# Attention scores computed by slot, with block transposes on VectorE, in a fused attention and two expert networks

## The chip, the cores and the metric
The kernel runs on one core of one Trainium2 chip. The metric is the device time of one execution in microseconds (us), the median of several runs.

## The reference
All inputs come in float32 but for the weights, which are float64; what is computed is this:

```python
a = phi - np.max(phi, axis=2, keepdims=True)          # phi: (8, 8, 576, 32)
a = np.exp(a); a = a / (np.sum(a, axis=2, keepdims=True) + 1e-09)
k_m = np.einsum('bhsm,bhsd->bhmd', a, k)              # k, v, q: (8, 8, 576, 64)
v_m = np.einsum('bhsm,bhsd->bhmd', a, v)
scores = np.matmul(q, k_m.transpose(0, 1, 3, 2)) / np.sqrt(64)
scores = scores - np.max(scores, axis=-1, keepdims=True)
attn = np.exp(scores)
attn = attn / (np.sum(attn, axis=-1, keepdims=True) + 1e-09)
x = np.matmul(attn, v_m)                              # tokens 4608 x 512
g = x @ w_gate
x = (g / (1 + np.exp(-g)) * (x @ w_val)) @ w_out      # 512 -> 1536 -> 512
h = x @ w_in                                          # 512 -> 2048 -> 512
out = np.where(h > 0, h, np.exp(np.minimum(h, 0)) - 1) @ w2_out
```

There are 8 batches of 8 heads, 576 tokens, head size 64 and 32 memory slots. For each head k and v are first pooled into 32 slots (k_m, v_m); the softmax over the slots is the attention.

## The kernel before
The program has three stages. Stage 1 goes over the batches; in each it computes units 0 to 3 of the first expert network (a unit is 128 of the 1536 hidden columns), in two halves of 288 tokens (HS). Stage 2 does units 4 to 11 of all batches, stage 3 the second expert network. The attention is spread over stage 1 only. v_m is never multiplied with the attention: it is folded into the gate and value weights (`vw`, L139, eight matmuls on 64x32 tiles of the array), so the gate and value matmuls (`gate1`, `val1`, L151 to L153) take the normalised scores `at`, split in a high and a low part. `down1` is L156 to L158. VectorE makes s (L176) and h (L183) from their PSUM tiles, which release the three banks of `ps_gv`, and the low part hl (L164).

The attention of a batch has two parts.
- `front_tasks`: `phi` (max L216 on VectorE, exp on ScalarE L219), `a_T` (transposes of the exponentials, by TensorE, L234, copied by ScalarE L236), `kv_mm` (L247: the products with k and v; two groups g of four heads j, each head a 32-column strip of the array, over five chunks of tokens of which the last has 64), `kv_out` (L255, the division by the sum) and `kv_T` (L263: transposes; ScalarE copies the v part to vt, L266, and the k part to kT, L271, into a tile padded with zeros by GpSimd, L270).
- `back_tasks`: `score` (L282: per chunk of 128 tokens and pair of heads one matmul with 128 tokens of q stationary and 64 columns of the padded kT moving; the result has tokens on partitions), max over slots L286, subtraction L287, exp L288, `norm` (sum L294, L295, reciprocal L296, product L297), and `attn_T` (L307: TensorE turns the normalised scores back to slots on partitions; ScalarE writes the high part, L310, VectorE the low part, L311). `score` and `norm` work on three pieces of two, two and one chunk, `attn_T` on two pieces.

In stage 1 the lists of tasks of later batches are worked off by `tick()` between gates, values and downs; ahead of it stand batch 0 and part of batches 1 and 2 in a prologue. A scheduler then sets the order on each engine. Every engine, and the DMA queue on SP, works in its own order; `together` keeps a group of matmuls next to each other. Weights come in float64 and are split by ScalarE (L100, L107), VectorE (L101 to L105) and GpSimd (L108 to L111). The buffers that count here: `ps_at` has two PSUM banks for scores and their transposes, `ps_fr` one, `kvr` six chunks (NKV), `qr` six chunks (NQ).

Of the kernel before, what the change touches and what calls it, by code (L numbers as in the profile page):

```python
# [37 lines left out]
def attention_moe_moe(ctx: ExitStack, tc: tile.TileContext, qT, phiT, kv, w1g, w1o, w2, out):
# [148 lines left out]
    ident = bk_p.tile([128, 128], F32, tag="ident", name="ident")  # L187
    make_identity(nc, ident)

    def chunk(c):  # L190
        return min(128, S - 128 * c)

    class Batch:
        def __init__(self, b):
# [5 lines left out]
            nc.sync.dma_start(out=self.ph, in_=phiT[self.b].rearrange("g p s -> p g s"))  # L200

        def load_kv(self, c):
            n = chunk(c)
            t = self.kvr[c] = fr_p.tile([128, 2, 512], F32, tag="kvr", name="kvr", bufs=NKV)
            nc.sync.dma_start(out=t[:n], in_=kv[self.b, 128 * c:128 * c + n])

        def load_q(self, c):
            n = chunk(c)
            t = self.qr[c] = bk_p.tile([128, 512], F32, tag="qr", name="qr", bufs=NQ)
            nc.sync.dma_start(out=t[:, :4 * n], in_=qT[self.b, :, 512 * c:512 * c + 4 * n])  # L210


        def phi(self):
# [8 lines left out]
            nc.vector.tensor_scalar_add(out=self.rs, in0=sm, scalar1=1e-9)  # L222
            nc.vector.reciprocal(out=self.rs, in_=self.rs)

        def a_T(self, c0):
# [2 lines left out]
            n = chunk(c0)
            nch = 2 if n == 128 else 1
            ps = ps_fr.tile([128, 2, 256], F32, tag="at", name="ps_aT")  # L230
            for i in range(nch):
                for g in range(2):
                    s0 = 128 * (c0 + i)
                    nc.tensor.transpose(out=ps[:n, i, 128 * g:128 * g + 128],  # L234
                                        in_=self.ph[:, g, s0:s0 + n], identity=ident)
            act(out=self.a[:n, c0:c0 + nch], in_=ps[:n, :nch], func=AF.Copy)  # L236


        def kv_mm(self, cs, start, stop):
            if start:  # L240
                self.kvp = [ps_kv.tile([128, 2, D], F32, tag="at", name="ps_kvm") for _ in range(2)]

            def head(c, g, j):
                n = chunk(c)
                t = self.kvr[c].rearrange("p t (j g d) -> p t g j d", j=4, g=2)
                o = 128 * g + 32 * j
                return mm(self.kvp[g][32 * j:32 * j + 32], lhsT=self.a[:n, c, o:o + 32], rhs=t[:n, :, g, j, :],  # L247
                          start=start and c == cs[0], stop=stop and c == cs[-1])
# [9 lines left out]
        def kv_T(self):  # L260
# [6 lines left out]
            self.kT = bk_p.tile([128, 4, 2, M], F32, tag="kT", name="kT", bufs=2)
            for g in range(2):
                r, o = slice(64 * g, 64 * g + 64), slice(64 - 64 * g, 128 - 64 * g)
                nc.gpsimd.memset(self.kT[o, :, g, :], 0.0)  # L270
                act(out=self.kT[r, :, g, :], in_=ps[r, 0], func=AF.Copy)  # L271


        def score(self, c0, c1):
            if c0 == 0:
                self.sc = bk_p.tile([128, NCH, 256], F32, tag="sc", name="sc")
            n, k = chunk(c0), (c1 - c0) * 8
            ps = ps_at.tile([128, 2, 2, 4, M], F32, tag="at", name="ps_sc")
            for c in range(c0, c1):
                q = self.qr.pop(c)[:, :4 * n].rearrange("p (j s) -> p j s", j=4)  # L280
                for j in range(4):
                    mm(ps[:n, c - c0, :, j, :], lhsT=q[:, j, :], rhs=self.kT[:, j], start=True, stop=True)  # L282
            p = ps[:n, :c1 - c0].rearrange("p c g j m -> p (c g j) m")
            sc = self.sc[:n, c0:c1, :].rearrange("p c (h m) -> p (c h) m", m=M)
            mx = bk_p.tile([128, 16, 1], F32, tag="mx", name="mx", bufs=2)[:n, :k]
            nc.vector.tensor_reduce(out=mx, in_=p, op=ALU.max, axis=AX.X)  # L286
            tt(out=sc, in0=p, in1=mx.to_broadcast([n, k, M]), op=ALU.subtract)  # L287
# [2 lines left out]
        def norm(self, c0, c1):  # L290
            n, k = chunk(c0), (c1 - c0) * 8
            sc = self.sc[:n, c0:c1, :].rearrange("p c (h m) -> p (c h) m", m=M)
            sm = bk_p.tile([128, 16, 1], F32, tag="smx", name="smx", bufs=2)[:n, :k]
# [3 lines left out]
            tt(out=sc, in0=sc, in1=sm.to_broadcast([n, k, M]), op=ALU.mult)  # L297

        def attn_T(self, c0, c1):
            if c0 == 0:  # L300
# [1 line left out]
            s0, s1 = 128 * c0, min(S, 128 * c1)
            for g in range(2):
                ps = ps_at.tile([128, 512], F32, tag="at", name="ps_atT")[:, :s1 - s0]
                for c in range(c0, c1):
                    n = chunk(c)
                    nc.tensor.transpose(out=ps[:, 128 * (c - c0):128 * (c - c0) + n],  # L307
                                        in_=self.sc[:n, c, 128 * g:128 * g + 128], identity=ident[:n, :n])
                hi, lo = self.at[:, 0, g, s0:s1], self.at[:, 1, g, s0:s1]
                a = act(out=hi, in_=ps, func=AF.Copy)  # L310
                self.mark = a, tt(out=lo, in0=ps, in1=hi.bitcast(F32), op=ALU.subtract)  # L311
# [19 lines left out]

    def back_tasks(b):
        z, nxt = Bs[b], Bs[b + 1] if b + 1 < B else None
        yield lambda: (z.score(0, 2), nxt and [nxt.load_q(c) for c in (0, 1)])
        yield lambda: (z.score(2, 4), nxt and [nxt.load_q(c) for c in (2, 3)])
        yield lambda: (z.score(4, 5), nxt and nxt.load_q(4), 0 < b < B - 2 and Bs[b + 2].phi())
        yield lambda: z.norm(0, 2)
        yield lambda: (z.attn_T(0, 2), setattr(z, 'mark1', z.mark))
        yield lambda: (z.norm(2, 4), z.norm(4, 5))
        yield lambda: (z.attn_T(2, 5), z.store_at())  # L340
# [276 lines left out]
```

## Time and profile before

| | us |
|---|---|
| median of 3 runs (lowest, highest) | 1632.61 (1631.53, 1634.37) |
| the profiled execution | 1629.19 |
| its span, first to last instruction | 1627.4 |
| TensorE busy | 1577.3 (97%) |
| VectorE busy | 962.4 (59%) |
| ScalarE busy | 659.3 (41%) |
| GpSimd busy | 169.4 (10%) |

The mean granted clock of TensorE is 0.982 of full speed. How to read it: the busy shares are means over three stages with different limits; what lies ahead of about 330 us holds all of the attention, and what follows has none. Busy time of TensorE counts overlapping matmuls once; the time of a group of matmuls is read from its start to the start of the next instruction. One fp32 matmul leaves two records in the trace.

### The profile page before, as it was taken

The numbers are of one execution on the slowest core, as the hardware profiler recorded it, in microseconds if no ns is written. First come the engines' busy times: TensorE is split into PE (matmuls) and PEld (weight loads), VectorE is DVE, ScalarE is ACT, GpSimd is POOL, SyncE is SP. The second block draws the span as 40 slices with busy tenths as digits, with TensorE's granted clock in tenths as the row PEclk, the third lists the DMA queues.
The fourth block names the chain that finished last, engine by engine and source line by source line (L and its number), as shares of the span: only waits on it lengthen the run. The fifth ranks groups of instructions, "written<-read, shape, count | busy, mean of one in ns | idle before, by whom it ended". The sixth has DMA issues, their size and how long they took to land.

```text
span 1627.4 us, 24651 instructions
## 1 busy us (share of the span) xinstructions
PE 1577.3 (97%) x9968; PEld 1358.8 (83%) x9968; DVE 962.4 (59%) x1718; ACT 659.3 (41%) x1281; POOL 169.4 (10%) x135
## 2 busy tenths in 40 slices
PE   6699999999999999999999999999999999999998
PEld 4588888888999999999987788888888888888887
DVE  5778777665444544443799755555555555555554
ACT  3455444454333333333455443434343434343333
POOL 1211111132011010100244200000000000000000
PEclk7699999999999999999999999999999999999999
DMA  8877443243222322221242010101010101010000
GB/s 300 272 251 251 166 140 133 76 167 108 73 94 82 101 74 83 85 87 45 87 149 91 34 33 0 52 1 52 1 52 1 52 0 53 1 52 0 26 1 26
DMA packets 65906, 136.34 MB, mean 84 GB/s; under 512 B 6912, under 2 KB 38656, under 8 KB 63744
## 3 DMA queue, kind: packets, MB, share of 16 engines
q1 hardware_dynamic: 56576, 125.32, 23.0%
q10 hardware_dynamic: 9216, 9.44, 1.7%
q8 instruction: 78, 1.28, 0.3%
q14 instruction: 36, 0.29, 0.1%
HBM read 96.99 MB, written 37.75 MB: 83 GB/s over the span
## 4 chain that ended last, share of the span: by engine, by line
PE 80%; DVE 9%; DMA 7%; ACT 2%; issue 1%; SPq 0%; ACTq 0%; DVEq 0%
PE pu L534 7%; PE pu L535 7%; PE pu L533 7%; PE acc L559 7%; PE acc L560 7%; PE acc L561 7%; PE acc L156 4%; PE acc L158 4%; PE acc L157 4%; PE pg L151 3%; PE pv L151 3%; PE pvw L139 3%; PE pg L153 3%; PE pg L152 3%; PE pv L152 2%; PE pv L153 2%
## 5 line engine op out<-in xcount | busy, mean ns | idle before, releaser
L561 PE MATMUL acc<-whi,hl 128*128 128x512 f32 x576 | 222.5, 391 | 2.8 <-DVE hl L164 2.8
L559 PE MATMUL acc<-whi,hh 128*128 128x512 f32 x576 | 224.3, 389 | 0.1
L560 PE MATMUL acc<-wlo,hh 128*128 128x512 f32 x576 | 224.1, 389 | 0.0
L533 PE MATMUL pu<-x1s,whi 128*128 128x512 f32 x576 | 224.1, 389 | 0.0
L534 PE MATMUL pu<-x1s,whi 128*128 128x512 f32 x576 | 224.1, 389 | 0.0
L535 PE MATMUL pu<-x1s,wlo 128*128 128x512 f32 x576 | 224.1, 389 | 0.0
L548 DVE SCALAR_TENSOR_TENSOR g<-e,g 128x512 f32<-128x512 f32 x144 | 103.7, 720 | 159.2 <-ACT g L547 159.2
L162 ACT ACTIVATE hh<-g 128x512 fp32r<-128x512 f32 x144 | 91.0, 632 | 212.8 <-DVE g L549 209.4
L183 DVE SCALAR_TENSOR_TENSOR h<-s,pv 128x288 f32<-128x288 f32 x192 | 86.5, 450 | 146.5 <-PE pv L153 132.5
L546 ACT ACTIVATE e<-g 128x512 f32<-128x512 f32 x144 | 90.8, 631 | 202.8 <-DVE g L545 202.8
L164 DVE TENSOR_TENSOR hl<-g,hh 128x512 fp32r<-128x512 f32 x144 | 101.1, 702 | 88.5 <-ACT hh L162 88.4
L156 PE MATMUL acc<-hh,whi 128*128 128x288 f32 x512 | 151.3, 296 | 0.1
L157 PE MATMUL acc<-hh,wlo 128*128 128x288 f32 x512 | 150.5, 294 | 0.0
L158 PE MATMUL acc<-hl,whi 128*128 128x288 f32 x512 | 149.5, 295 | 0.0
L162 ACT ACTIVATE hh<-h 128x288 fp32r<-128x288 f32 x192 | 85.0, 443 | 153.1 <-DVE h L183 152.6
L164 DVE TENSOR_TENSOR hl<-h,hh 128x288 fp32r<-128x288 f32 x192 | 94.5, 492 | 65.0 <-ACT hh L162 65.0
L561 PEld LDWEIGHTS acc<-whi,hl 128*128 128x128 f32 x576 | 108.0, 188 | 28.5 <-DVE hl L164 6.2
L559 PEld LDWEIGHTS acc<-whi,hh 128*128 128x128 f32 x576 | 108.2, 188 | 22.7 <-ACT hh L162 0.5
L534 PEld LDWEIGHTS pu<-x1s,whi 128*128 128x128 f32 x576 | 108.3, 188 | 22.4
L560 PEld LDWEIGHTS acc<-wlo,hh 128*128 128x128 f32 x576 | 108.0, 188 | 22.4
L533 PEld LDWEIGHTS pu<-x1s,whi 128*128 128x128 f32 x576 | 108.1, 188 | 22.3
L535 PEld LDWEIGHTS pu<-x1s,wlo 128*128 128x128 f32 x576 | 108.1, 188 | 22.3
(85 smaller groups left out, 3281.2 us busy)
## 6 DMA issues: line engine op xcount, KB each, us to landing
kvr<-kv SPq DMA_DIRECT2D x32, 512.0 KB, 7.5
wr<-w SPq DMA_DIRECT2D x32, 512.0 KB, 3.5
wr<-w1g SPq DMA_DIRECT2D x24, 512.0 KB, 4.7
atd<-at SPq DMA_DIRECT2D x8, 1152.0 KB, 4.7
p1d<-p ACTq DMA_DIRECT2D x64, 144.0 KB, 1.8
p1l<-p1d SPq DMA_DIRECT2D x16, 576.0 KB, 4.2
at<-atd SPq DMA_DIRECT2D x8, 1152.0 KB, 5.2
x1d<-p1l SPq DMA_DIRECT2D x16, 576.0 KB, 3.3
```

Source lines behind the costliest of these rows:

```text
L156: mm(ps, lhsT=w[0][:, ms], rhs=hs[0], start=start, stop=False)
L157: mm(ps, lhsT=w[1][:, ms], rhs=hs[0], start=False, stop=False)
L158: mm(ps, lhsT=w[0][:, ms], rhs=hs[1], start=False, stop=stop)
L162: act(out=hh, in_=h, func=AF.Copy)
L164: tt(out=hl, in0=h, in1=hh.bitcast(F32), op=ALU.subtract)
L533: mm(ps, lhsT=wh[:, k, :], rhs=xh, start=k == 0, stop=False)
L534: mm(ps, lhsT=wh[:, k, :], rhs=xl, start=False, stop=False)
L535: mm(ps, lhsT=wl[:, k, :], rhs=xh, start=False, stop=k == KD - 1)
L548: stt(out=g, in0=e, scalar=1.0, in1=g, op0=ALU.add, op1=ALU.mult)
L559: mm(accs[c], lhsT=hs[0][:, cs], rhs=wh, start=u == 0, stop=False)
L560: mm(accs[c], lhsT=hs[0][:, cs], rhs=wl_, start=False, stop=False)
L561: mm(accs[c], lhsT=hs[1][:, cs], rhs=wh, start=False, stop=u == NU2 - 1)
```

## The change
- `score` works by half (288 tokens) in place of by chunk. Now kT of a head is stationary (64 x 32) and q moves with 288 columns: eight heads lie side by side on eight 64x32 tiles of the array, into two PSUM tiles with slots on partitions. kT is no longer padded.
- VectorE turns the scores in blocks of 32x32 into an SBUF tile (two instructions of 128x288 a half), then max, subtraction, exp, sum, reciprocal and product run on 128x576; one more block transpose of 128x576 turns them back (into `ex`), and the high and low parts come from there. `attn_T` with its TensorE transposes is gone.
- The second group of phi comes rolled by 64 tokens, so the last 64 tokens of both groups share one transpose and one tile; the last 64 tokens of k and v come packed (`kv4`), so their eight matmuls are on 64x32 tiles.
- The loop of `kv_mm` has j outside and g inside, where g was outside.
- NKV is 5 (and two small `kv4` buffers), NQ is 3 halves; two transfers of q a batch in place of five; `back_tasks` has six tasks in place of seven.

```diff
-NKV = 6
-NQ = 6
+NKV = 5
+NQ = 3
...
         def a_T(self, c0):
             if c0 == 0:
-                self.a = fr_p.tile([128, NCH, 256], F32, tag="a", name="a")
...
+                self.a = fr_p.tile([128, 9, 128], F32, tag="a", name="a")
+            ps = ps_fr.tile([128, 4, 128], F32, tag="at", name="ps_aT")
+            ph = self.ph.rearrange("p g s -> p (g s)")
+            if c0 == 4:
+                nc.tensor.transpose(out=ps[:, 0], in_=ph[:, 512:640], identity=ident)
+                act(out=self.a[:, 8], in_=ps[:, 0], func=AF.Copy)
+                return
...
             def head(c, g, j):
...
+                if c < 4:
+                    a = self.a[:, 2 * c + g, col]
+                    t = self.kvr[c].rearrange("p (t j g d) -> p g j t d", t=2, j=4, g=2)[:, g, j]
+                else:
+                    r = slice(64 * g, 64 * g + 64)
+                    a, t = self.a[r, 8, col], self.kvr[c][r].rearrange("p (t j d) -> p j t d", t=2, j=4)[:, j]
+                return mm(self.kvp[g][col], lhsT=a, rhs=t, start=start and c == cs[0], stop=stop and c == cs[-1])
...
-            together([lambda c=c, g=g, j=j: head(c, g, j) for c in cs for g in (1, 0) for j in range(4)])
+            together([lambda c=c, g=g, j=j: head(c, g, j) for c in cs for j in range(4) for g in (1, 0)])
...
+        def score(self, hf):
+            q = self.qr.pop(hf)
+            ps = [ps_at.tile([128, HS], F32, tag="at", name="ps_sc") for _ in range(2)]
+
+            def head(j, g):
+                r = slice(64 * g, 64 * g + 64)
+                return mm(ps[g][32 * j:32 * j + 32], lhsT=self.kT[r, j, :], rhs=q[r, j, :], start=True, stop=True)
+
+            together([lambda j=j, g=g: head(j, g) for j in range(4) for g in (1, 0)])
+            t = self.sc = bk_p.tile([128, 2, HS], F32, tag="sc", name="sc", bufs=2)
             for g in range(2):
...
+                nc.vector.transpose(out=t[:, g], in_=ps[g])
+            sc = t.rearrange("p g (b m) -> p (g b) m", m=M)
+            mx = bk_p.tile([128, 2 * HS // M, 1], F32, tag="mx", name="mx", bufs=2)
+            nc.vector.tensor_reduce(out=mx, in_=sc, op=ALU.max, axis=AX.X)
+            tt(out=sc, in0=sc, in1=mx.to_broadcast([128, 2 * HS // M, M]), op=ALU.subtract)
             act(out=sc, in_=sc, func=AF.Exp, scale=1.0 / float(D) ** 0.5)
...
+        def attn(self, hf):
+            if hf == 0:
                 self.at = av_p.tile([128, 2, 2, S], F32R, tag="at", name="at")
...
+            t = bk_p.tile([128, 2, HS], F32, tag="ex", name="ex")
+            nc.vector.transpose(out=t.rearrange("p g s -> p (g s)"), in_=self.sc.rearrange("p g s -> p (g s)"))
+            hi, lo = (self.at[:, i, :, HS * hf:HS * hf + HS] for i in range(2))
+            a = act(out=hi, in_=t, func=AF.Copy)
+            self.mark = a, tt(out=lo, in0=t, in1=hi.bitcast(F32), op=ALU.subtract)
```

The order on the engines shows how the work moves at two places. On TensorE, between the pooling of batch 1 and the first gate (L139 at the end is the second vw group of batch 0; the first gate follows it), there stood before:

```order
L139 MATMUL pvw<-wg,vt 32x512 x8
L263 MATMUL ps_kvT<-ident,kvm 128x128 x2
L234 MATMUL ps_aT<-ident,ph 128x128 x4
L282 MATMUL ps_sc<-kT,qr 128x2x32 x11
L234 MATMUL ps_aT<-ident,ph 128x128 x4
L282 MATMUL ps_sc<-kT,qr 128x2x32 x5
L282 MATMUL ps_sc<-kT,qr 64x2x32 x4
L234 MATMUL ps_aT<-ident,ph 64x128 x2
L247 MATMUL ps_kvm<-kvr,a 32x128 x40
L307 MATMUL ps_atT<-ident,sc 128x128 x4
L139 MATMUL pvw<-wg,vt 32x512 x8
```

And now:

```order
L265 MATMUL ps_kvT<-ident,kvm 128x128 x2
L139 MATMUL pvw<-wg,vt 32x512 x8
L280 MATMUL ps_sc<-qr,kT 32x288 x8
L235 MATMUL ps_aT<-ident,ph 128x128 x4
L280 MATMUL ps_sc<-qr,kT 32x288 x8
L235 MATMUL ps_aT<-ident,ph 128x128 x4
L229 MATMUL ps_aT<-ident,ph 128x128
L251 MATMUL ps_kvm<-kvr,a 32x128 x40
L265 MATMUL ps_kvT<-ident,kvm 128x128 x2
L280 MATMUL ps_sc<-qr,kT 32x288 x8
L235 MATMUL ps_aT<-ident,ph 128x128 x4
L139 MATMUL pvw<-wg,vt 32x512 x8
```

The scores of batch 1 are two groups of eight in place of twenty matmuls in pieces, L307 is gone, and the kv transposes, half of the scores and four of the transposes of the next batch now stand ahead of the first gate.

On VectorE, at the softmax of batch 1 (L101 to L105 are the splitting of weights), there stood before:

```order
L286 TENSOR_REDUCE mx<-ps_sc 128x16
L287 TENSOR_TENSOR sc<-ps_sc,mx 128x512
L101 TENSOR_SCALAR wc<-wv 128x512
L102 SCALAR_TENSOR_TENSOR wv<-wv,wc 128x512
L294 TENSOR_REDUCE smx<-sc 128x16
L104 TENSOR_SCALAR wc<-wv 128x512
L101 TENSOR_SCALAR wc<-wv 128x512
L295 TENSOR_SCALAR smx<-smx 128x16
L105 SCALAR_TENSOR_TENSOR wc<-wr,wc 128x512
L102 SCALAR_TENSOR_TENSOR wv<-wv,wc 128x512
L296 RECIPROCAL smx<-smx 128x16
L286 TENSOR_REDUCE mx<-ps_sc 128x16
```

And now:

```order
L285 STREAM_TRANSPOSE sc<-ps_sc 128x288 x2
L101 TENSOR_SCALAR wc<-wv 128x512
L288 TENSOR_REDUCE mx<-sc 128x18
L102 SCALAR_TENSOR_TENSOR wv<-wv,wc 128x512
L289 TENSOR_TENSOR sc<-sc,mx 128x576
L285 STREAM_TRANSPOSE sc<-ps_sc 128x288
L104 TENSOR_SCALAR wc<-wv 128x512
L285 STREAM_TRANSPOSE sc<-ps_sc 128x288
L101 TENSOR_SCALAR wc<-wv 128x512
L105 SCALAR_TENSOR_TENSOR wc<-wr,wc 128x512
L295 TENSOR_REDUCE smx<-sc 128x18
L288 TENSOR_REDUCE mx<-sc 128x18
```

The max no longer reads PSUM but the tile that two block transposes have filled; those alone release the score banks.

## Rows read from the trace of the kernel before

**Rows 1.** Windows: busy us (x count) by engine, granted clock, DMA share, GB/s.
```profile
core 0: us, PE busy (x) PEld busy (x) DVE busy (x) ACT busy (x) POOL busy (x), PEclk, DMA share, GB/s
60.00:80.00 20.00, 13.22 (x129) 9.42 (x128) 18.02 (x37) 8.82 (x21) 7.90 (x8) 0.68 0.77 246
80.00:100.00 20.00, 17.44 (x195) 14.97 (x194) 19.43 (x40) 9.85 (x24) 6.85 (x7) 0.91 0.80 278
120.00:320.00 200.00, 194.13 (x1649) 169.05 (x1648) 151.27 (x331) 93.55 (x218) 23.65 (x23) 0.99 0.46 155
220.00:240.00 20.00, 17.96 (x124) 14.39 (x117) 17.11 (x36) 9.23 (x21) 3.86 (x5) 0.91 0.34 115
420.00:1627.00 1207.00, 1197.62 (x6750) 1030.81 (x6748) 669.80 (x1106) 466.44 (x838) 94.52 (x62) 1.00 0.15 50
```

**Rows 2.** Waits of TensorE, 120 to 320 us: us in total, times, longest.
```profile
PE pd L156 <- DVE h L183: 3.7, 3, 2.0
```

**Rows 3.** Timeline of TensorE in the middle: start us, us, engine, line, form, count.
```profile
187.17 2.52 PE L247 MATMUL ps_kvm<-kvr,a 64*32 64x128 f32 x80
189.63 0.40 PE L156 MATMUL pd<-hh,whi 128*128 128x288 f32 x1
...
202.34 0.58 PE L307 MATMUL ps_atT<-ident,sc 128*128 128x128 f32 x3
202.85 0.40 PE L151 MATMUL pv<-at,vw 128*128 128x288 f32 x1
203.09 0.29 PE L152 MATMUL pv<-at,vw 128*128 128x288 f32 x1
...
206.75 1.00 PE L282 MATMUL ps_sc<-kT,qr 128*128 128x64 f32 x8
207.56 0.38 PE L151 MATMUL pv<-at,vw 128*128 128x288 f32 x1
207.78 0.29 PE L152 MATMUL pv<-at,vw 128*128 128x288 f32 x1
```

**Rows 4.** Timeline of TensorE around one vw group in stage 2.
```profile
419.76 0.29 PE L152 MATMUL pv<-at,vw 128*128 128x288 f32 x1
419.89 0.29 PE L153 MATMUL pv<-at,vw 128*128 128x288 f32 x1
420.12 1.09 PE L139 MATMUL pvw<-wg,vt 64*32 64x512 f32 x16
421.13 0.40 PE L156 MATMUL acc<-hh,whi 128*128 128x288 f32 x1
421.37 0.29 PE L157 MATMUL acc<-hh,wlo 128*128 128x288 f32 x1
```

**Rows 5.** Timeline of TensorE in the prologue.
```profile
18.42 8.14 PE L282 MATMUL ps_sc<-kT,qr 128*128 128x64 f32 x40 [1.95 <-ACT kT L271]
...
75.14 1.90 PE L307 MATMUL ps_atT<-ident,sc 128*128 128x128 f32 x6 [3.42 <-DVE at L311]
```

**Rows 6.** VectorE by line and form, 0 to 420 us: busy us, mean ns, idle before.
```profile
L286 DVE TENSOR_REDUCE mx<-ps_sc 128x16 f32<-128x512 f32 x16 | 10.9, 680 | 5.7 <-PE ps_sc L282 5.7
L311 DVE TENSOR_TENSOR at<-ps_atT,at 128x320 fp32r<-128x320 f32 x16 | 7.8, 488 | 1.5 <-ACT at L310 1.5
L311 DVE TENSOR_TENSOR at<-ps_atT,at 128x256 fp32r<-128x256 f32 x16 | 6.4, 417 | 1.2 <-ACT at L310 0.9 <-DMA p1d<-p 0.3
L255 DVE TENSOR_SCALAR kvm<-ps_kvm,rs 128x128 f32<-128x128 f32 x16 | 4.7, 328 | 7.1 <-PE ps_kvm L247 7.1
L286 DVE TENSOR_REDUCE mx<-ps_sc 64x8 f32<-64x256 f32 x8 | 3.3, 407 | 0.0
L296 DVE RECIPROCAL smx<-smx 64x8 f32<-64x8 f32 x8 | 1.4, 174 | 0.0
```

More of the change, by code (lines that the diff above doesn't have):

```diff
@@ L32, with attention_moe_moe @@
 NWC = 8
-NKV = 6
-NQ = 6
+NKV = 5
+NQ = 3
 @with_exitstack
-def attention_moe_moe(ctx: ExitStack, tc: tile.TileContext, qT, phiT, kv, w1g, w1o, w2, out):
+def attention_moe_moe(ctx: ExitStack, tc: tile.TileContext, qT, phiT, kv, kv4, w1g, w1o, w2, out):
     nc = tc.nc
@@ L188, in attention_moe_moe @@
     make_identity(nc, ident)
-    def chunk(c):
-        return min(128, S - 128 * c)
     class Batch:
@@ L202, in load_kv, with load_q @@
         def load_kv(self, c):
[L203 to L210, printed above, removed]
+            t = self.kvr[c] = fr_p.tile([128, 1024 if c < 4 else 512], F32, tag="kvr" if c < 4 else "kv4",
+                                        name="kvr", bufs=NKV if c < 4 else 2)
+            nc.sync.dma_start(out=t, in_=kv[self.b, 128 * c:128 * c + 128] if c < 4 else kv4[self.b])
+        def load_q(self, hf):
+            t = self.qr[hf] = bk_p.tile([128, 4, HS], F32, tag="qr", name="qr", bufs=NQ)
+            nc.sync.dma_start(out=t, in_=qT[self.b, hf].rearrange("p (j s) -> p j s", j=4))
         def phi(self):
@@ L226, in a_T @@
             if c0 == 0:
-                self.a = fr_p.tile([128, NCH, 256], F32, tag="a", name="a")
[L228 to L231, printed above, removed]
+                self.a = fr_p.tile([128, 9, 128], F32, tag="a", name="a")
[5 more added lines that the diff above has]
+                return
+            for i in range(2):
                 for g in range(2):
[L233 to L236, printed above, removed]
+                    s0 = 128 * (c0 + i) + 640 * g
+                    nc.tensor.transpose(out=ps[:, 2 * i + g], in_=ph[:, s0:s0 + 128], identity=ident)
+            act(out=self.a[:, 2 * c0:2 * c0 + 4], in_=ps, func=AF.Copy)
         def kv_mm(self, cs, start, stop):
@@ L243, in head @@
             def head(c, g, j):
[L244 to L248, printed above, removed]
-            together([lambda c=c, g=g, j=j: head(c, g, j) for c in cs for g in (1, 0) for j in range(4)])
+                col = slice(32 * j, 32 * j + 32)
+                if c < 4:
[6 more added lines that the diff above has]
+            together([lambda c=c, g=g, j=j: head(c, g, j) for c in cs for j in range(4) for g in (1, 0)])
         def kv_out(self):
@@ L264, in kv_T @@
                                     in_=self.kvm[:, i].rearrange("p g d -> p (g d)"), identity=ident)
+            self.kT = bk_p.tile([128, 4, M], F32, tag="kT", name="kT", bufs=2)
+            act(out=self.kT, in_=ps[:, 0], func=AF.Copy)
             self.vt = vt_p.tile([128, 4, M], F32, tag="vt", name="vt")
             act(out=self.vt, in_=ps[:, 1], func=AF.Copy)
[L267 to L271 removed]
@@ L274, in score @@
[L274 to L287, printed above, removed]
+        def score(self, hf):
[6 more added lines that the diff above has]
+            t = self.sc = bk_p.tile([128, 2, HS], F32, tag="sc", name="sc", bufs=2)
+            for g in range(2):
+                nc.vector.transpose(out=t[:, g], in_=ps[g])
[3 more added lines that the diff above has]
+            tt(out=sc, in0=sc, in1=mx.to_broadcast([128, 2 * HS // M, M]), op=ALU.subtract)
@@ L288, in score, with norm @@
             act(out=sc, in_=sc, func=AF.Exp, scale=1.0 / float(D) ** 0.5)
[L290 to L293, printed above, removed]
+        def norm(self, hf):
+            sc = self.sc.rearrange("p g (b m) -> p (g b) m", m=M)
+            sm = bk_p.tile([128, 2 * HS // M, 1], F32, tag="smx", name="smx", bufs=2)
@@ L296, in norm @@
             nc.vector.reciprocal(out=sm, in_=sm)
-            tt(out=sc, in0=sc, in1=sm.to_broadcast([n, k, M]), op=ALU.mult)
-        def attn_T(self, c0, c1):
-            if c0 == 0:
+            tt(out=sc, in0=sc, in1=sm.to_broadcast([128, 2 * HS // M, M]), op=ALU.mult)
+        def attn(self, hf):
+            if hf == 0:
                 self.at = av_p.tile([128, 2, 2, S], F32R, tag="at", name="at")
[L302 to L311, printed above, removed]
+            t = bk_p.tile([128, 2, HS], F32, tag="ex", name="ex")
[3 more added lines that the diff above has]
+            self.mark = a, tt(out=lo, in0=t, in1=hi.bitcast(F32), op=ALU.subtract)
         def store_at(self):
@@ L333, in back_tasks @@
         z, nxt = Bs[b], Bs[b + 1] if b + 1 < B else None
[L334 to L340, printed above, removed]
+        yield lambda: z.score(0)
+        yield lambda: (z.norm(0), nxt and nxt.load_q(0))
+        yield lambda: (z.attn(0), setattr(z, 'mark1', z.mark))
+        yield lambda: (z.score(1), 0 < b < B - 2 and Bs[b + 2].phi())
+        yield lambda: (z.norm(1), nxt and nxt.load_q(1))
+        yield lambda: (z.attn(1), z.store_at())
     G2 = [(ps_gv, "g")] * 2
@@ L355, in attention_moe_moe @@
         Bs[0].load_kv(c)
-    for c in range(NCH):
-        Bs[0].load_q(c)
+    for hf in range(2):
+        Bs[0].load_q(hf)
     Bs[0].phi()
@@ L593 @@
     gate, val = (inputs[n].reshape(KD, 128, NU1 // 2, 2, 1, 128) for n in ("moe_w_gate", "moe_w_val"))
+    ph = phi.reshape(B, 4, 2, S, M).transpose(0, 2, 1, 4, 3).reshape(B, 2, 128, S)
+    kvn = np.stack([a.transpose(0, 2, 1, 3).reshape(B, S, DM) for a in (k, v)], axis=2)
     arrays = {
-        "qT": np.concatenate([qT[..., c:c + 128].reshape(B, 128, -1) for c in range(0, S, 128)], axis=2),
-        "phiT": phi.reshape(B, 4, 2, S, M).transpose(0, 2, 1, 4, 3).reshape(B, 2, 128, S),
-        "kv": np.stack([k.transpose(0, 2, 1, 3).reshape(B, S, DM), v.transpose(0, 2, 1, 3).reshape(B, S, DM)], axis=2),
+        "qT": qT.reshape(B, 128, 4, 2, HS).transpose(0, 3, 1, 2, 4).reshape(B, 2, 128, 4 * HS),
+        "phiT": np.stack([ph[:, 0], np.roll(ph[:, 1], 64, axis=2)], axis=1),
+        "kv": kvn[:, :512].reshape(B, 512, 1024),
+        "kv4": kvn[:, 512:].reshape(B, 64, 2, 4, 2, D).transpose(0, 4, 1, 2, 3, 5).reshape(B, 128, 512),
         "w1g": np.concatenate([gate, val], axis=4).transpose(2, 0, 1, 3, 4, 5).reshape(NU1 // 2, KD, 128, 512),
```

## The prediction, made before the changed kernel ran
> **What bounds the kernel now.** I read the windows first. From 420 us to the end TensorE is busy 1197.62 of 1207 us [rows 1]: units 4 to 11 and the second expert network run there, the change touches nothing of them, and I take that stretch as fixed. All of the attention lies before about 330 us. In 120 to 320 us TensorE is busy 194.13 of 200 us and VectorE 151.27; so TensorE sets the pace there, and VectorE has 48.7 us to spare. The list of waits agrees: the largest wait of TensorE there is 3.7 us, for VectorE's h [rows 2]. Before 100 us it is otherwise. In 60 to 80 us TensorE is busy only 13.22 of 20 us and VectorE 18.02; in 80 to 100 us VectorE is busy 19.43; the transfers take 0.77 to 0.80 of their engines' time [rows 1]. So the prologue is paced by VectorE and the transfers, the middle by TensorE. TensorE work that goes is worth its full length in the middle and only a part of it in the prologue; VectorE work that comes costs little in the middle and much in the prologue.
>
> **TensorE, per batch.**
> Scores before: 40 records per batch (20 fp32 matmuls, two records each). Eight of them run from 206.75 to 207.56 us, 0.81 us, so 0.101 each [rows 3], 4.05 a batch; at half clock, batch 0 shows 8.14 us for 40 [rows 5]. They come in about six pieces, and behind a piece the first large matmul takes 0.22 us to the next one (207.56 to 207.78) and not 0.13: 0.09 each, 0.54. Together 4.6 us.
> Scores after: two groups of eight, on 64x32 tiles with 288 columns moving. The nearest row is the vw group: eight matmuls on 64x32 tiles with 512 columns, 1.01 us from 420.12 to 421.13 [rows 4]. By columns a group is 288/512 of that, 0.57 (if nothing of it is fixed; with all of it fixed 1.01, the other bound). I take the first, since kv's 80 records in four strips give 2.46/20 = 0.123 us for a record of 128 columns [rows 3], and the vw group, two records on each of its eight tiles, 1.01/2 = 0.505 for 512: in proportion to columns. At each end the array changes its tiling: 0.23 us from the last large matmul to the group, and 0.24 behind it, against 0.13 between large ones [rows 4]; so 0.10 twice. A group is 0.77, a batch 1.55: **-3.05** (with 1.01 instead of 0.57: -2.2).
> [...]
> Transposes of the normalised scores (ten a batch): three take from 202.34 to 202.85 us, 0.17 each, 1.7, and 0.11 behind each of some four pieces (202.85 to 203.09) [rows 3]: **-2.06**, all of it.
> kv: the last 64 tokens are one fifth of 2.46 us (187.17 to 189.63) [rows 3], 0.49; eight abreast instead of four halves that at best: between 0 and -0.25, I take **-0.12**. One transpose of a less: **-0.17**. The new order of the kv matmuls (both groups g of a column strip in a row) I cost at nothing, because the two records of one matmul, which share a strip, already stand side by side in the order before; see the first rival.
> Sum -5.4 us a batch. The scores and transposes of batches 3 to 7 lie in the middle: 5 x 5.4 = **-27.0**.
>
> **VectorE, per batch.** Each of the passes max, subtract, sum and multiply goes from three instructions to two of 576 elements. From the two max rows, 2 x 0.680 + 0.407 = 1.767 becomes 2 x 0.75 (0.680, plus 64 elements at the slope 0.488 - 0.417 = 0.071 of the lo rows) = 1.50 [rows 6]: -0.27 each, and the lo split, 2 x 0.417 + 2 x 0.488 = 1.81 to 2 x 0.77, the same. Five times: -1.35; two small instructions go with the third piece, the reciprocal 0.174 [rows 6] and the addition ahead of it, counted alike: -0.35. Added: four block transposes of 128x288 and two of 128x576. No row shows one. At the price of other instructions of that length (0.417 at 256, 0.488 at 320, so 0.45; and 0.75) they are 4 x 0.45 + 2 x 0.75 = 3.3. Below: 128 elements cost 0.328 [rows 6], so 0.33 each, 2.0; above I put twice, 6.6. I take 3.3, since a transpose reads and writes as many elements as a copy. Net **+1.6** (0.3 to 4.9).
> [...]
>
> ScalarE and GpSimd only lose instructions (copies of pieces, two memsets a batch); neither bounds, I cost both at nothing. DMA bytes are the same in fewer, larger transfers on the same queue: nothing.
>
> **What is given back in the middle.** VectorE rises from 151.3 by 5 x 1.6 to 159.3 while TensorE falls from 194.1 to 167.1. Where weights are split it gets tight: in 220 to 240 us VectorE is busy 17.11 and TensorE 17.96 [rows 1]; after, some 17.9 against 15.3. At the share of 80 to 100 us (19.43 of 20) such a piece lasts 18.4: 1.1 us more than 15.3 and today's 2.0 of idling, in each of five batches. **+6** (0 to half the gain, 13.5).
>
> **Prologue.** Batches 0 to 2 lose 3 x 5.4 = 16.2 us on TensorE, of which I count half, -8, as it waits there for VectorE (3.42 us at 75.14 [rows 5]) and transfers. VectorE has 3 x 1.6 = 4.8 more and is at its limit: +4.8. The order shows score work of batch 2 ahead of the first gate that stood behind it, so VectorE gets more, earlier, but none of it is extra. **-3.5** (-12 with everything kept, +6 with nothing of it and VectorE's load in full).
>
> Sum: -27.0 + 6 - 3.5 = -24.5 on the profiled 1629.2 us: 1604.7. The median of the runs lies 3.4 above the profiled one: **1608 us**. What this kernel's runs can tell from no change is 0.2%, 3.3 us.
>
> **Rivals.**
> (A) The kv order halves the overlap: if two matmuls of one strip must follow one another and block those behind, only two of four strips work, and the 32 full-height matmuls take 1.97 us more a batch: 5 x 1.97 + 3 for the prologue = +13, 1621. For it: nothing in the trace has four records of one strip in a row. Against: pairs do no harm. 0.13.
> (B) Slower: TensorE waits for h and s. VectorE works in order, and a 0.75 us transpose may stand ahead of the row that frees a gate's PSUM bank; with VectorE at 159 of some 175 us its queue is seldom empty. Such a wait is about 2 us, and in 220 to 240 us it comes with the granted clock down to 0.91 [rows 1], 1.8 us more: 3.8 in all. The gain of 24.5 is gone with 6.5 waits beyond those counted; with nine in five batches the time is 1642. Against: in 120 to 320 us there are three such waits [rows 2] at 76% load. 0.11.
> (C) All eight batches keep the whole 5.4 us, VectorE is hidden everywhere: -43, 1589. Against it the prologue's windows. 0.10.
> (D) The change doesn't do what it says: the two row halves of a score group run one after the other, +1.14 a batch, some +8 in all: 1616. Against it the vw row. 0.10.
> (E) Block transposes cost twice the rows: VectorE +4.9 a batch, 175.8 in the middle; that stretch then can't be under 175.8/0.97 = 181 and gains 19, the prologue loses 3 x 4.9 - 8 = 6.7: -12.3, 1620. 0.12.
>
> **How the numbers follow.** The forecast has 0.44. The range 1594 to 1631 holds it, A, D and E, and leaves out most of B and C. Faster by over 0.2%: forecast and C, D whole, nine tenths of A and E, 0.85 by that; I give 0.80, as several terms stack. Within 0.2%: 0.09; slower, B: 0.11.
>
> **What would show it.** Right: no matmul for score transposes; a score group of eight under 0.8 us from start to next matmul; kv still 2.3 to 2.5 us; block transposes near 0.45 and 0.75; TensorE's busy time down by some 40 us, and the first steady stretch reached a few us sooner. Wrong: kv over 3 us (A); many waits of L156 or L151 for VectorE and clock below 0.95 in the middle (B); transposes of 0.9 and 1.5 us (E); groups over 1.1 us (D).

## The result and the profile after

The changed kernel takes 1611.99 us (median of 4 runs, 1610.99 to 1612.53) against 1632.73 us: ratio 0.9872, 95% interval 0.9855 to 0.9889, so 20.7 us or 1.3% faster. A second set of five runs gave 0.9872 again (0.9853 to 0.9892). The forecast was 1608, range 1594 to 1631. The two profiled executions lie closer together than the medians, 1629.19 and 1611.78 us, because the profiled one of before was among its fastest; where traces are compared below, the difference is 17.4 us.

The first line of the page after says what went:

```profile
PE 1538.0 (96%) x9816; PEld 1313.0 (82%) x9816; DVE 971.6 (60%) x1702; ACT 653.7 (41%) x1249; POOL 166.5 (10%) x119
```

TensorE was busy 1577.3 us before, so 39.3 us of its work are gone; the forecast was "some 40". The span fell by only 17.4 us: TensorE idles 22 us more than before. The windows show where; the columns are those of [rows 1], and three windows of 20 us are added.

```profile
60.00:80.00 20.00, 12.48 (x83) 7.89 (x83) 20.00 (x37) 9.55 (x20) 6.69 (x5) 0.59 0.79 286
80.00:100.00 20.00, 14.74 (x171) 9.84 (x171) 20.00 (x38) 9.93 (x24) 6.29 (x5) 0.76 0.71 257
120.00:140.00 20.00, 19.13 (x225) 14.94 (x223) 20.00 (x44) 10.01 (x25) 2.09 (x2) 1.00 0.85 318
140.00:160.00 20.00, 18.88 (x202) 16.30 (x201) 12.48 (x27) 11.11 (x26) 3.38 (x3) 1.00 0.62 216
160.00:180.00 20.00, 17.76 (x219) 14.41 (x218) 19.22 (x43) 8.63 (x20) 2.56 (x2) 1.00 0.58 198
120.00:320.00 200.00, 185.60 (x1628) 159.19 (x1626) 163.81 (x335) 96.62 (x216) 30.51 (x22) 0.98 0.46 162
220.00:240.00 20.00, 17.28 (x124) 16.90 (x130) 14.30 (x28) 8.38 (x19) 3.25 (x3) 0.91 0.32 110
```

Between 60 and 100 us VectorE is busy without a break and TensorE for 27.2 of 40 us, where it was 30.7. In the middle VectorE now alternates between full stretches (20.00, 19.22) and looser ones, and TensorE is idle for 14.4 of 200 us where it was 5.9. The four largest waits of TensorE from 120 to 320 us, to be read like [rows 2]:

```profile
PE pvw L139 <- DVE s L176: 3.6, 4, 2.2
PE pv L151 <- DVE vw L144: 3.2, 2, 2.7
PE pd L156 <- DVE h L183: 2.5, 2, 1.2
PE pg L151 <- DVE s L176: 1.8, 3, 1.2
```

All four are waits for VectorE. TensorE's timeline has the new groups at full clock (1.00 granted in both stretches), to be read like [rows 3]; the time of a group is from its start to the next start.

```profile
106.02 2.40 PE L251 MATMUL ps_kvm<-kvr,a 64*32 64x128 f32 x80
108.35 0.40 PE L151 MATMUL pv<-at,vw 128*128 128x288 f32 x1
...
202.03 0.29 PE L158 MATMUL pd<-hl,whi 128*128 128x288 f32 x1
202.26 0.71 PE L280 MATMUL ps_sc<-qr,kT 64*32 64x288 f32 x16
202.90 0.40 PE L151 MATMUL pg<-at,vw 128*128 128x288 f32 x1
203.14 0.30 PE L152 MATMUL pg<-at,vw 128*128 128x288 f32 x1
```

A score group takes 0.64 us, kv 2.33 in place of 2.46, and behind a group the first large matmul costs 0.24, as before. Ahead of a group there is 0.23 from the last large matmul (202.03 to 202.26), where ahead of the old full-array groups it was 0.13 to 0.14. VectorE by line and form, 0 to 420 us, to be read like [rows 6]:

```profile
L285 DVE STREAM_TRANSPOSE sc<-ps_sc 128x288 f32<-128x288 f32 x32 | 13.8, 461 | 0.2
L298 DVE TENSOR_TENSOR sc<-sc,smx 128x576 f32<-128x576 f32 x16 | 13.1, 816 | 0.1
L308 DVE TENSOR_TENSOR at<-ex,at 128x576 fp32r<-128x576 f32 x16 | 13.0, 814 | 0.1
L289 DVE TENSOR_TENSOR sc<-sc,mx 128x576 f32<-128x576 f32 x16 | 12.9, 805 | 0.0
L305 DVE STREAM_TRANSPOSE ex<-sc 128x576 f32<-128x576 f32 x16 | 12.3, 770 | 0.0
L288 DVE TENSOR_REDUCE mx<-sc 128x18 f32<-128x576 f32 x16 | 11.9, 741 | 0.0
```

**Where the time went.** The time of the h instructions (L183) marks the progress through the gates: there are 192 of them, in the same sequence in both kernels. The first, the 9th, the 17th and the 49th stand in VectorE's timeline before at

```profile
82.22 0.44 DVE L183 SCALAR_TENSOR_TENSOR h<-s,pv 128x288 f32<-128x288 f32 x1
...
119.19 0.46 DVE L183 SCALAR_TENSOR_TENSOR h<-s,pv 128x288 f32<-128x288 f32 x1
...
163.96 0.46 DVE L183 SCALAR_TENSOR_TENSOR h<-s,pv 128x288 f32<-128x288 f32 x1
...
322.00 0.44 DVE L183 SCALAR_TENSOR_TENSOR h<-s,pv 128x288 f32<-128x288 f32 x1
```

and after at

```profile
83.33 0.44 DVE L183 SCALAR_TENSOR_TENSOR h<-s,pv 128x288 f32<-128x288 f32 x1
...
123.04 0.44 DVE L183 SCALAR_TENSOR_TENSOR h<-s,pv 128x288 f32<-128x288 f32 x1
...
164.29 0.44 DVE L183 SCALAR_TENSOR_TENSOR h<-s,pv 128x288 f32<-128x288 f32 x1
...
304.14 0.45 DVE L183 SCALAR_TENSOR_TENSOR h<-s,pv 128x288 f32<-128x288 f32 x1
```

At the 9th h, one batch of gates in, the changed kernel is 3.9 us late. Up to the 17th, two batches in, nothing is gained (+0.3 us); between the 17th and the 49th it is 18.2 us, and behind that the two run alike to within 2 us. The windows between the marks, TensorE's score matmuls alone, before (L282) and after (L280), tell why (columns: TensorE busy, weight loads busy, clock, DMA share, GB/s):

```profile
0.00:164.00 164.00, 25.89 (x160) 24.98 (x160) 0.83 0.79 268
164.00:322.00 158.00, 20.66 (x160) 19.43 (x160) 0.99 0.37 126
```
```profile
0.00:164.30 164.30, 10.76 (x160) 2.83 (x160) 0.82 0.76 281
164.30:304.10 139.80, 4.29 (x96) 1.09 (x96) 0.98 0.37 126
```

Forty records before, and 32 after, are a batch. At the 17th h the old kernel had done four batches of scores, the new one five: 160 of 256 records. Scheduler and buffers let the attention run ahead of the gates, and by my reading the first part of the gain went here: into work done ahead, not into time. All engines up to the 9th h and from there to the 49th, and over the same two stretches as above (before, then after; columns as in [rows 1]):

```profile
0.00:119.19 119.19, 88.24 (x829) 70.94 (x829) 82.85 (x174) 52.13 (x121) 24.64 (x33) 0.77 0.80 274
119.19:322.00 202.81, 196.94 (x1666) 171.39 (x1665) 154.03 (x334) 95.07 (x222) 24.85 (x23) 0.99 0.45 154
0.00:164.00 164.00, 132.12 (x1291) 109.91 (x1292) 118.14 (x250) 75.80 (x177) 30.54 (x39) 0.83 0.79 268
164.00:322.00 158.00, 153.05 (x1205) 132.42 (x1204) 118.73 (x258) 71.40 (x165) 18.95 (x17) 0.99 0.37 126
```
```profile
0.00:123.04 123.04, 76.81 (x845) 52.92 (x846) 95.96 (x182) 52.88 (x114) 23.54 (x23) 0.76 0.79 293
123.04:304.14 181.10, 168.35 (x1493) 143.15 (x1491) 147.25 (x310) 87.98 (x196) 21.36 (x16) 0.98 0.44 154
0.00:164.30 164.30, 116.09 (x1286) 85.71 (x1290) 129.67 (x255) 75.65 (x168) 29.01 (x27) 0.82 0.76 281
164.30:304.10 139.80, 129.07 (x1058) 110.36 (x1050) 113.51 (x237) 65.17 (x142) 15.89 (x12) 0.98 0.37 126
```

To the 17th h TensorE has 16.0 us less to do and VectorE 11.5 more, the softmax of one more batch among it; the time is the same. Behind it, where TensorE was busy 153 of 158 us, TensorE has 24.0 us less to do and VectorE 5.2 less, and 18.2 us come out as time. The batch moved ahead is part of both differences. From the 9th to the 49th h TensorE has 28.6 us less to do, idles 6.9 more, and 21.7 come out.

### The profile page after: what moved, and what is told of

The parts are those of the page before. It is cut to its first block, busy times and chain, and to the rows that moved or that the text cites. A ratio compares the mean times of both kernels' runs of the same rounds, so it can differ in the third digit from the quotient of the medians.

```text
span 1610.0 us, 24209 instructions
## 1 busy us (share of the span) xinstructions
PE 1538.0 (96%) x9816; PEld 1313.0 (82%) x9816; DVE 971.6 (60%) x1702; ACT 653.7 (41%) x1249; POOL 166.5 (10%) x119
## 4 chain that ended last, share of the span: by engine, by line
PE 78%; DVE 12%; DMA 5%; ACT 3%; issue 2%; ACTq 0%; SPq 0%; DVEq 0%
PE pu L529 8%; PE pu L531 8%; PE pu L530 8%; PE acc L556 7%; PE acc L555 7%; PE acc L557 7%; PE acc L156 4%; PE acc L158 4%; PE acc L157 4%; PE pg L151 3%; DMA wr<-w1g 3%; PE pv L151 3%; PE pg L153 2%; PE pg L152 2%; PE pv L153 2%; PE pv L152 2%
## 5 line engine op out<-in xcount | busy, mean ns | idle before, releaser
L183 DVE SCALAR_TENSOR_TENSOR h<-s,pv 128x288 f32<-128x288 f32 x192 | 86.4, 450 | 145.1 <-PE pv L153 131.1
L541 DVE TENSOR_SCALAR g<-pu 128x512 f32<-128x512 f32 x144 | 99.3, 690 | 53.0 <-PE pu L531 52.9
L151 PE MATMUL pg<-at,vw 128*128 128x288 f32 x384 | 120.0, 312 | 7.7 <-DVE h L183 4.0
```

What stands on the lines that cost most here:

```text
L151: mm(ps, lhsT=wh, rhs=ah, start=g == 0, stop=False)
```

## The experiments

Two theories stand against each other on what bounds the attention's part of the changed kernel. V: VectorE sets the pace in the prologue and in every second 20 us of the middle. T: TensorE or the transfers do. A third came with the runs, O: any edit lets the scheduler set another order, and that alone moves the time. Every ratio is against the kernel before, run beside it; a difference to the changed kernel is the difference of the ratios (its own is 0.9872) times 1632 us. Each ratio is known to about 0.2%, 3 us, so a difference of two to about 4 us. The runs of one kernel differ by more: those of the kernel before go from 1627.01 to 1638.35 us, with a mean granted clock of 0.984 in the shortest and 0.975 in the longest. A trace is one run, and its marks carry this spread too.

| run | edit to the changed kernel | ratio, interval | against the changed kernel, us |
|---|---|---|---|
| e1 | VectorE -13 us, GpSimd +24 | 0.9941 (0.9922 to 0.9960) | +11.3 |
| e2 | VectorE +4.6 early | 0.9918 (0.9898 to 0.9938) | +7.5 |
| e3 | VectorE +7.7 late | 0.9929 (0.9910 to 0.9947) | +9.3 |
| e4 | the packing alone, on the kernel before | 1.0014 (0.9998 to 1.0030) | |
| e5 | VectorE -25 | 0.9812 (0.9793 to 0.9830) | -9.8 |
| e6 | VectorE -5 | 0.9884 (0.9865 to 0.9903) | +2.0 |
| e7 | kv loop order | 0.9896 (0.9875 to 0.9916) | +3.9 |
| e8 | TensorE +10 | 0.9904 (0.9884 to 0.9923) | +5.2 |
| e9 | none | 0.9872 (0.9853 to 0.9892) | 0 |
| e10 | VectorE -5.5, ScalarE more | 0.9871 (0.9851 to 0.9892) | -0.2 |
| e11 | VectorE -10, ScalarE more | 0.9893 (0.9872 to 0.9914) | +3.4 |
| e12 | scores alone, without the packing | 0.9885 (0.9868 to 0.9901) | +2.1 |

### One part alone: e4 and e12

e4 is the kernel before with phi rolled, nine transposes, `kv4` and the new kv order; scores, their transposes and q as before. Its diff is shown in part, and so is that of e12.

```diff
-NKV = 6
+NKV = 5
...
-            together([lambda c=c, g=g, j=j: head(c, g, j) for c in cs for g in (1, 0) for j in range(4)])
+            together([lambda c=c, g=g, j=j: head(c, g, j) for c in cs for j in range(4) for g in (1, 0)])
...
+        "kv4": kvn[:, 512:].reshape(B, 64, 2, 4, 2, D).transpose(0, 4, 1, 2, 3, 5).reshape(B, 128, 512),
```

> The kernel before with the packed last 64 tokens (phi rolled, kv4, nine transposes) and the new kv order alone; scores and their transposes as before. From the terms of the prediction, 0.3 us a batch on TensorE, of which batches 3 to 7 count: -1 to -3 against the kernel before. Rival A (the kv order halves the overlap): +8 or more, with kv near 4 us. A third reading, that the packing carries a large share of the gain: -6 or more.

No difference is seen: 1.0014, which is +2.3 us (-0.3 to +4.9), so the 1 to 3 us that were expected did not show. Its kv runs in 2.33 us, as in the changed kernel:

```profile
116.30 2.40 PE L255 MATMUL ps_kvm<-kvr,a 64*32 64x128 f32 x80
118.63 0.40 PE L151 MATMUL pg<-at,vw 128*128 128x288 f32 x1
```

So rival A is out; the 0.13 us a batch are there in the trace, and they are too few to show in the time. e12 is the other half: the changed kernel with phi, kv, their buffers and their loop order taken back.

```diff
-NKV = 5
+NKV = 6
...
-            together([lambda c=c, g=g, j=j: head(c, g, j) for c in cs for j in range(4) for g in (1, 0)])
+            together([lambda c=c, g=g, j=j: head(c, g, j) for c in cs for g in (1, 0) for j in range(4)])
```

> The scores by slot with VectorE's block transposes alone; phi, kv and their last 64 tokens, the kv loop order and their buffers as in the kernel before. If the scores carry all of the gain (the packing alone gave none): ratio 0.985 to 0.990 to the kernel before, the same as the whole change within the 4 us by which neutral edits moved it. If the two parts need each other: above 0.992.

0.9885: the scores carry the gain, within what these runs resolve.

### More and less work on VectorE: e2, e3, e5

```diff
-            nc.vector.transpose(out=t.rearrange("p g s -> p (g s)"), in_=self.sc.rearrange("p g s -> p (g s)"))
+            for _ in range(2 if self.b < 3 else 1):
+                nc.vector.transpose(out=t.rearrange("p g s -> p (g s)"), in_=self.sc.rearrange("p g s -> p (g s)"))
```

> The block transpose back (128x576, 0.77 us) is issued twice in batches 0 to 2 only: 6 x 0.77 = 4.6 us more on VectorE in the prologue, the same result. Theory V: +3 to +5, 1615 to 1617. Rival T: 0 to +1, 1612 to 1613.

e3 has `self.b >= 3` in its place.

> The same doubling in batches 3 to 7 only: 10 x 0.77 = 7.7 us more on VectorE in the middle. Theory V: about half of it shows, +3 to +5, 1615 to 1617. Rival T: 0 to +1, 1612 to 1613.

The costs are +7.5 for 4.6 and +9.3 for 7.7, each known to about 4 us: the work that was put in, and perhaps more. The 17th and the 49th h tell where the cost falls. In e2 (164.29 and 304.14 in the changed kernel):

```profile
170.22 0.44 DVE L183 SCALAR_TENSOR_TENSOR h<-s,pv 128x288 f32<-128x288 f32 x1
...
310.42 0.45 DVE L183 SCALAR_TENSOR_TENSOR h<-s,pv 128x288 f32<-128x288 f32 x1
```

and in e3:

```profile
164.15 0.42 DVE L183 SCALAR_TENSOR_TENSOR h<-s,pv 128x288 f32<-128x288 f32 x1
...
316.48 0.42 DVE L183 SCALAR_TENSOR_TENSOR h<-s,pv 128x288 f32<-128x288 f32 x1
```

e2 is 5.9 us late at the first mark and 6.3 at the second, e3 in time at the first and 12.3 late at the second (the trace of e3 is of its longest run, 1622.57 us). T, which expected at most 1, is out by e3. e2 alone would not show it: e7 below, with nothing added to VectorE, is 4.5 us late at the first mark. From the first h to the 17th e2 takes 87.8 us at a granted clock of 0.92, e7 86.7 at 0.92, and the changed kernel 81.0 at 0.95. In e3 too a lower clock goes with the cost: 0.94 between the marks, in place of 0.98. e5 goes the other way: max and subtraction are left out, so the exponentials are of the raw scores.

```diff
-            mx = bk_p.tile([128, 2 * HS // M, 1], F32, tag="mx", name="mx", bufs=2)
-            nc.vector.tensor_reduce(out=mx, in_=sc, op=ALU.max, axis=AX.X)
-            tt(out=sc, in0=sc, in1=mx.to_broadcast([128, 2 * HS // M, M]), op=ALU.subtract)
```

> The changed kernel without the max over slots and its subtraction (left out; the exponentials are taken of the raw scores): VectorE loses 4 x 0.77 = 3.1 us a batch, 25 us in all, TensorE nothing. After the first runs doubling cost 1.4 us for each us of VectorE. Theory V (VectorE sets the pace in the prologue and in every second 20 us of the middle): 10 to 20 us under the changed kernel, 1592 to 1602, until TensorE bounds the middle again. Theory O (what the first three runs showed is the scheduler's other order, not VectorE's time): anything within 8 us on either side of the changed kernel.

25 us less on VectorE give 9.8, and 10.3 of them are there at the 49th h (293.81 us). In its middle VectorE has 44 us free and TensorE is busy 189.41 us, in place of 185.60:

```profile
120.00:320.00 200.00, 189.41 (x1678) 161.29 (x1677) 155.57 (x321) 100.12 (x224) 30.81 (x22) 1.00 0.46 160
```

So work added to VectorE in the middle counts about in full, work taken away by 0.4 (0.2 to 0.6): the changed kernel stands close to where VectorE's pace and TensorE's meet.

### More work on TensorE: e8

```diff
-            together([lambda j=j, g=g: head(j, g) for j in range(4) for g in (1, 0)])
+            together([lambda j=j, g=g: head(j, g) for _ in range(2) for j in range(4) for g in (1, 0)])
```

> Each group of score matmuls is issued twice into the same banks, the same result: TensorE has 16 x 0.65 = 10 us more (more at half clock), VectorE the same. Theory V: TensorE has slack in the prologue and where VectorE paces; +2 to +5, 1614 to 1617. Rival T (TensorE sets the pace throughout the middle): +6 to +10, 1618 to 1622.

+5.2, at the upper end of V and below T's range: about half of what is added to TensorE counts. With 4 us either way this run alone does not tell V from T.

### Small reliefs of VectorE, and another order: e1, e6, e7, e9, e10, e11

```diff
-            self.mark = a, tt(out=lo, in0=t, in1=hi.bitcast(F32), op=ALU.subtract)
+            self.mark = a, nc.gpsimd.tensor_tensor(out=lo, in0=t, in1=hi.bitcast(F32), op=ALU.subtract)
```

> The low part of the attention (128x576, 0.81 us on VectorE, twice a batch) goes to GpSimd; all else is as in the changed kernel. Theory V (VectorE now sets the pace of the prologue and of every second 20 us in the middle): 16 x 0.81 = 13 us leave VectorE, of which the prologue's 4.9 count nearly in full and the middle's 8.1 by about half: 7 to 10 us under the changed kernel, 1602 to 1605. Rival T (TensorE or the transfers set the pace, VectorE's busy windows are only work done early): within 2 us of the changed kernel, 1610 to 1614. Rival G (GpSimd's longer instruction comes onto the path of the first gate): slower than 1614.

Slower by 11.3 us: V's sign is wrong here. The low part takes 1.51 us on GpSimd (0.81 on VectorE), and GpSimd also ends the splitting of every weight (L111) in its own order. In the first 420 us of e1 this line of TensorE's waits is new, and the low part's group on GpSimd shows its length:

```profile
PE pvw L139 <- POOL wg L111: 3.4, 1, 3.4
```
```profile
L308 POOL TENSOR_TENSOR at<-ex,at 128x576 fp32r<-128x576 f32 x16 | 24.2, 1512 | 96.4 <-ACT at L307 73.1 <-issue 23.3
```

VectorE's own weight instructions grew as well: L101 from a mean of 548 to 641 ns, while its median stays at 420. The growth is in the longest ones (up to 1.66 us). The trace of the changed kernel has long ones of this line too, without any change of order: seven in the first 420 us take 0.72 to 1.37 us, each lies beside a GpSimd instruction (L108, L109 or L111), and ends 0.27 to 0.29 us after it. Another line's is shown in the next section. So this VectorE instruction was longer beside GpSimd's work in these traces; how much of the 11.3 us that makes is not shown, as the order of e1 changed as well. Rival G of that expectation holds as to the result.

e6 drops the additions of 1e-9, this one and that in phi:

```diff
-            nc.vector.tensor_scalar_add(out=sm, in0=sm, scalar1=1e-9)
```

> The changed kernel without the additions of 1e-9 (three small VectorE instructions a batch, 0.21 us each in the scores, 0.29 in phi; the sums are at least 1, so float32 loses nothing): 5 us less on VectorE in all. Theory V: 3 to 6 under the changed kernel, 1606 to 1609. Theory O: unforeseeable, within 8 us on either side.

e7 turns the kv loop back:

```diff
-            together([lambda c=c, g=g, j=j: head(c, g, j) for c in cs for j in range(4) for g in (1, 0)])
+            together([lambda c=c, g=g, j=j: head(c, g, j) for c in cs for g in (1, 0) for j in range(4)])
```

> The changed kernel with the old loop order of the kv matmuls (g outside, j inside). Rival A of the prediction (the new order halves the overlap) fell by the trace, where 40 kv matmuls take 2.33 us; so by the matmuls nothing changes: within 2 us of the changed kernel. The scheduler moves pieces of the scores between the first gates in this version; theory O: this alone moves the time by 3 us or more.

Its kv takes 2.27 us in one piece:

```profile
119.76 2.33 PE L251 MATMUL ps_kvm<-kvr,a 64*32 64x128 f32 x80
122.03 0.40 PE L151 MATMUL pg<-at,vw 128*128 128x288 f32 x1
```

The matmuls are no slower, yet the ratio is 3.9 us above the changed kernel's, with other neighbours on TensorE (one score group is cut in two by transposes). The intervals of the two overlap, and the six runs of e7, all of one order, go from 1609.77 us (clock 0.982) to 1618.04 (0.976): its shortest is as short as those of the changed kernel. So it is not shown that another order costs 3.9 us, nor any. e9 is the changed kernel again:

> The changed kernel once more, as the point of comparison beside the next two on the same chip: ratio to the kernel before 0.987 as at first (0.9855 to 0.9889).

e10 moves the scaling of k and v to ScalarE, and e11 drops the additions as well:

```diff
-                nc.vector.tensor_scalar(out=self.kvm[:, :, g, :], in0=self.kvp[g], scalar1=self.rs[:, g:g + 1],
-                                        scalar2=None, op0=ALU.mult)
+                act(out=self.kvm[:, :, g, :], in_=self.kvp[g], func=AF.Copy, scale=self.rs[:, g:g + 1])
```

> The changed kernel with the division of the pooled k and v by their sums (two instructions a batch, 0.34 us each on VectorE) on ScalarE, as a copy with a scale per partition: 16 x 0.34 = 5.5 us leave VectorE, and TensorE's transposes of kv, which waited 12 us for these two in the first 120 us, no longer stand behind weights and softmax in VectorE's order. Theory V: 4 to 10 under the changed kernel. Theory O (small edits only reshuffle): within 4 us on either side.

> Both small reliefs of VectorE: kv scaled on ScalarE, and no additions of 1e-9, 10 us less on VectorE in all. Theory V: 6 to 12 under the changed kernel, 1600 to 1606. Theory O: within 4 us of it on either side.

e6, e10 and e11 took 5 to 10 us from VectorE and changed nothing for the better: +2.0, -0.2, +3.4. V in its strong form, a us for a us, is refuted by them; at 0.4 (e5) they should have gained 2 to 4, which the 4 us of error would hide. The traces of e6 and e11 do show a gain and its loss: at the 17th h they are 3.1 and 5.1 us ahead of the changed kernel, at the 49th 1.5 behind and level, with a granted clock of 0.96 and 0.94 in between, where it was 0.98. What remains of V is one-sided: more VectorE work costs, less of it soon stops paying. How much of a difference of 4 to 8 us is VectorE, order, clock or chance can't be told from these runs: it would need kernels with the same order on every engine, and more runs of each, which were not tried. No version with the whole softmax beat the changed kernel beyond its interval.

## Why the prediction was right, and which of its terms were not

The time, the sign and the mechanism of the middle held: 1608 forecast, 1612 measured; profile against profile, -24.5 forecast and -17.4 measured. The 7 us between them are the prologue's, below.

- **Scores, -3.05 a batch.** A group was put at 0.57 plus 0.10 at each end, 0.77; it takes 0.64 from start to start, 0.10 more ahead of it and 0.11 behind it (202.90 to 203.14 in place of 0.13), 0.85, so the term is -2.9. By columns was nearly the right reading of the vw row [rows 4], and rival D is out. The prediction put the 0.10 at both ends down to the change of tiling; the old full-array groups cost 0.09 to 0.11 behind them too [rows 3] and nothing ahead, so only the 0.10 ahead goes with the tiles.
- **Transposes, -2.06; kv, -0.12; a, -0.17.** L307 is gone; kv lost 0.13. (1.7 and four times 0.11 make 2.14, not 2.06.) The sum over the program is 39.3 us, where eight batches at 5.4 us make 43; the stretches near half clock in the prologue (granted 0.50 from 20 to 40 us before, 0.59 after) make this sum rough.
- **VectorE, +1.6 a batch.** The block transposes cost 0.461 and 0.770, forecast 0.45 and 0.75: the nearest rows were right, and rival E is out. Together they took 3.4 us a batch, forecast 3.3. The other passes were put at 0.75 to 0.77 each, and that is what most instructions take: the medians are 0.742 to 0.750. The means of subtraction, product and low part are higher, 0.805 to 0.816, as one of each sixteen or so takes 1.8 us. In all three lines the long one lies beside a GpSimd instruction and ends some 0.6 us after it, as here:

```profile
L289 DVE TENSOR_TENSOR sc<-sc,mx x16: 715/748/1812, 22.4 to 276.2; 128x576 f32<-128x576 f32 x16
```
```profile
72.34 1.31 POOL L109 TENSOR_TENSOR wlo<-wv,wc 128x512 fp32r<-128x512 f32 x1 [0.69 <-DVE wc L105]
72.45 1.81 DVE L289 TENSOR_TENSOR sc<-sc,mx 128x576 f32<-128x576 f32 x1
```

  (The first row gives shortest, median and longest in ns.) Before, the subtraction and the low part read PSUM, and the longest took 0.692 and 0.493 us. With small instructions that shrank by 0.20 and not 0.35, the attention's lines went from 80.9 to 96.2 us on VectorE, +1.9 a batch. Its busy time in the whole program rose by 9.2 us only, as the splitting of weights took less (L104: 31.1 to 28.1).
- **The middle: -27 and 6 given back, so -21.** The 9th h stands where the prediction begins the middle (119.19 us before, 120 in the prediction). From there to the 49th TensorE has 28.6 us less to do, idles 6.9 more, and 21.7 are gained. That is close, and in part by luck: the work is not that of the five batches which the term counts, as the new kernel has 112 of 256 score records behind this mark, three and a half batches, and the old one 200 of 320, five.
- **The prologue, -3.5.** This step failed, and with it the forecast missed by 7 us: at the 9th h the changed kernel is 3.9 us late, not 3.5 early. The prediction counted half of TensorE's relief of 16.2 us as time and 4.8 us more on VectorE (-8.1 + 4.8 is -3.3, not -3.5). By the windows up to the 9th h TensorE was relieved by 11.4 us (88.24 to 76.81 busy), but VectorE had 13.1 more (82.85 to 95.96) and was busy without a break from 60 to 100 us, as the attention ran further ahead (144 of 256 score records at this mark, four and a half batches, where the old kernel had 120 of 320, three). In the first 120 us TensorE's waits for VectorE's division of k and v (L258) went from 5.4 to 12.0 us; but those for ScalarE's exponentials of phi went from 8.2 to 14.2, and the transfers were busy for 0.71 to 0.79 from 60 to 100 us, so that VectorE alone holds the prologue is argued and not shown. The prediction says that earlier work on VectorE is "none of it extra"; that is true of the sum, but work ahead takes the time before the mark, and it came back only when the attention ended sooner.
- **Rival B** has its signs in the trace (four kinds of waits for VectorE lead the list; the clock is down to 0.91 in 220 to 240 us, as it was before), but at 8.5 us more of idle time from 120 to 320 us, not at the more than 24 from which it decides. e3 shows that more VectorE work in the middle would have begun to tip it.

## What to carry to other kernels

A gain on the engine that bounds is worth its length only while no other engine comes level: add up the other engines' work for the shortened stretch, not for the old one. Where tasks run ahead of their use, look for the gain at the end of the run-ahead, not where the work was removed. And before believing a small difference, look at the spread of one kernel's own runs; here it was 8 us among six runs of e7 and 11 among those of the kernel before, longer where the mean granted clock was lower (1609.77 us at 0.982 and 1618.04 at 0.976 in e7, 1627.01 at 0.984 and 1638.35 at 0.975 before).

## What the runs showed of the hardware that was not expected

A block transpose in 32x32 blocks on VectorE costs about what another instruction of its length does: 461 ns for 288 float32 columns out of PSUM, where h (L183, 128x288) has a mean of 447 ns, and 770 ns for 576 within SBUF, where the max and the sum (L288, L295) have 741 and 739. That makes (770 - 461) / 288 = 1.07 ns for a column more, if the source makes no difference. Two points can't show that the time per column is constant.

Moving the softmax from PSUM to SBUF did not make its passes cheaper. The subtraction, two operands of 128x576 in SBUF, has a median of 748 ns after, 1.30 ns a column; from PSUM before it was this row, 1.33 ns a column, and the mean of 805 is raised by the one long instruction beside GpSimd. From PSUM the longest of this line took 0.69 us, from SBUF 1.81:

```profile
L287 DVE TENSOR_TENSOR sc<-ps_sc,mx 128x512 f32<-128x512 f32 x16 | 10.9, 680 | 0.1
```
